# Storing a quarter of the output's rows in one transfer instead of four

## The chip, the cores and the metric

The kernel runs on one core of a Trainium2 chip. The core has a matrix engine (PE, with a separate row PEld for its weight loads), a vector engine (DVE), a scalar engine (ACT), GpSimd (POOL) and SyncE (SP). Data between the chip's buffers and DRAM moves through 16 DMA engines, which serve transfers issued from the queues of SP, ACT and POOL.

The metric is device time in microseconds of one execution. The profile is of one execution, and its span reaches from the first to the last instruction of the program.

## The reference

The kernel mixes two long convolutions of the same input with a gate. Shapes: one sequence of 2048 positions with 448 channels, bf16.

```python
x = A_u                                             # (1, 2048, 448)
g = sigmoid((x * gate_w).sum(-1, keepdims=True))    # a gate for each position
# A: state-space convolution; its kernel K is made from 256 complex modes a channel
K = einsum("dn,dnl,dn->dl", C, exp(dt * A * l), dt * B).real
a = irfft(rfft(x, 4096) * rfft(K, 4096))[:2048] + x * Dskip
# B: shifted keys times values, convolved with a given kernel, times x
kv = shift4(k, shift_k) * v
b = x * (irfft(rfft(kv, 4096) * rfft(ssm_k, 4096))[:2048] + kv * ssm_D)
return g * a + (1 - g) * b                          # (1, 2048, 448)
```

## The kernel before, in words

The two convolutions are done as Fourier transforms written as matrix products on PE. The 448 channels are held as 4 groups of 112; the work goes through four parts H = 0 to 3, each with 28 channels of every group. `PLAN` gives the order of the parts' steps: tables for the kernel of A (`table`), the convolution B (`conv_B`), the convolution A (`conv_A`), and the mixing of a finished part (`mix`). Parts 0 to 2 end in `mix`; part 3 ends in `end`, which also stores the output.

The order of the instructions is written out by hand. All calls on the engines are recorded in a list (`Order`), and `issue` replays them in the order that the string `ORDER` names by number; on each engine the instructions stand in that order. Since every call is replayed from line 144, nearly all rows of the profile carry L144, and groups are told apart by the names of their tiles. The strings `SLOTS` and `ROOMS` say which buffer each temporary uses, and `SIDES` says whether a copy out of PSUM is done by DVE (a TENSOR_SCALAR) or by ACT (an ACTIVATE).

The output's 2048 rows are seen as 32 x 4 x 16, named a, x and y: row = 64a + 16x + y. Two buffers called `lines`, each of 128 partitions, collect finished rows. Partition 32x + a holds, for that a and x, eight values of y with 448 channels each: `lines[0]` has y from 0 to 7 (q_82 in the program), `lines[1]` has y from 8 to 15 (q_80). So a partition's four neighbouring values of y are 4 x 448 x 2 = 3,584 bytes that are contiguous in the buffer and in the output.

`mix` fills the columns of parts 0 to 2. `end` goes over h = 0, 1 (the buffer) and k = 0, 1 (the half of its eight values of y). Each of the four passes does the last products of A on PE, gates and adds on DVE (tile RK), turns the result to the output's order on PE (`relay`, 16 small products), copies it out of PSUM with a change of sign (`evac.minus`), and stores that quarter of the rows. In the order as replayed the quarters are finished as h=1 k=0, then h=0 k=1 and h=1 k=1, then h=0 k=0; ACT does the copy of the first three, DVE that of the last.

The stores are issued from `dmae`, a list of SP and ACT. A store waits for the copies that write its rows, and nothing waits for a store but the end of the program. Every transfer signals on one of eight semaphores that are used in turn for SP's and ACT's transfers, and a transfer that takes up a semaphore waits for the transfer that used it before.

Of the kernel before, what the change touches and what calls it, by code (L numbers as in the profile page):

```python
# [110 lines left out]
)  # L111

def after(tc, ins, before):
# [55 lines left out]
def shaped(flat, shape, dtype=bf16, at=0):  # L169
    n = 1  # L170
    for s in shape:
        n *= s
    ap = flat if dtype is flat.dtype else flat.bitcast(dtype)
    ap = ap[:, at:at + n]
    names = "abcde"[:len(shape)]
    return ap.rearrange("p (%s) -> p %s" % (" ".join(names), " ".join(names)), **dict(zip(names, shape))) if len(shape) > 1 else ap
# [524 lines left out]
class Modes:  # L701
# [5 lines left out]
    def across(self, nm, put):  # L707
        for hf in range(2):
            for g in range(4):
                put(hf, g, self.raw[nm][:, g, hf * 128:(hf + 1) * 128])  # L710
# [36 lines left out]
def body(  # L747
# [22 lines left out]
    dmae = [nc.sync, nc.scalar]  # L770
# [143 lines left out]
    for b0 in range(0, 64, 8):  # L914
        pt = places.room()
        for i in range(2):
            for d in (0, -1, 1, -2, 2, -3, 3):
                t0 = b0 + 4 * i + d
                j0, j1 = max(0, -d), min(4, 4 - d)
                for g in range(4):  # L920
                    x = kT[g][:, t0 % 16, 2 + t0 // 16:2 + t0 // 16 + 4 * 31 + 1:4]
# [35 lines left out]
    out_rows = out[0].rearrange("(a x y) l -> x a y l", a=32, x=4)  # L957
    lines = []

    def line(y0):  # L960
        if not lines:
            lines.extend(qt([8, 448]) for _ in range(2))
        return lines[y0 // 8][:, y0 % 8:]

    def relay(o, g, part, first, last):
        for x in range(4):
            nc.tensor.matmul(o[32 * x:32 * x + 32].rearrange("p (y c) -> p y c", c=NC), lhsT=minus[:, 32 * g:32 * g + 32], rhs=part(x),
                             start=first, stop=last, tile_position=(0, 32 * x))

    def laid(t, H):  # L970
        return t.rearrange("p y (g h c) -> p h g y c", g=4, c=NC)[:, H]
# [8 lines left out]
    def end(U, H):  # L980
        across = lambda t, y0, n: t.rearrange("p (x y) c -> p x y c", x=4)[:, :, y0:y0 + n]
        for h in range(2):
            for k in range(2):
                ps, pt = (places.room()[:, 0] for _ in range(2))
                y0 = 8 * h + 4 * k
                b = across(ug[H], y0, 4)
                nc.tensor.matmul(ps[:, 0:448].rearrange("p (x y c) -> p x y c", x=4, c=NC), lhsT=minus[:], rhs=b, start=True, stop=False)
                for i in range(16):
                    for r in range(2):
                        l = 16 * (i // 4) + y0 + i % 4  # L990
                        nc.tensor.matmul(ps[:, i * NC:(i + 1) * NC], lhsT=G[:, l, r].rearrange("p g a -> p (g a)"), rhs=U[:, r, l],
                                         start=False, stop=(r == 1 and i == 15))
                t = shaped(arena["RK"][:], [4, 4, NC], at=448 * (2 * h + k))
                V.tensor_tensor(out=t, in0=ps[:, 0:448].rearrange("p (x y c) -> p x y c", x=4, c=NC),
                                in1=gt[:].rearrange("p (x y) -> p x y", x=4)[:, :, y0:y0 + 4].unsqueeze(3).to_broadcast([P, 4, 4, NC]), op=ALU.mult)
                V.tensor_tensor(out=t, in0=t, in1=b, op=ALU.add)
                for g in range(4):
                    relay(pt[:, 112 * g:112 * g + 112], g, lambda x: t[:, x], g == 0, g == 3)
                evac.minus(laid(line(y0)[:, 0:4], H), pt[:, 0:448].rearrange("p (g y c) -> p g y c", g=4, c=NC))
                for x in range(4):  # L1000
                    dmae[x % 2].dma_start(out_rows[x][:, y0:y0 + 4], lines[h][32 * x:32 * x + 32, 4 * k:4 * k + 4])

    held_open = []

# [50 lines left out]
    def conv_A(what, H, K):  # L1055
        X = spread_in(lambda c: uu[:, :, H * NC + c])
        transform(nc, places, W2, X, evac)
        X, S = swapped(X)
        if H < NQG - 1:
            transform(nc, places, W2, K, evac)  # L1060
            conv(products(nc, X, S, K), what, H)
            return
        U = qt([2, 64, NC])
        for c0 in (0, CB):
            transform(nc, places, W2, K, evac, c0, c0 + CB)
            for k0 in (0, 16):
                products(nc, X, S, K, k0, k0 + 16, c0, c0 + CB)
            stage_a(nc, places, R, whole(U, evac), (X, S), [range(c0, c0 + 8), range(c0 + 8, c0 + CB)])
        end(U, H)
# [57 lines left out]
```

## Time and profile before

| | before |
|---|---|
| time, median of 3 runs | 247.13 us (246.75 to 247.59) |
| the profiled execution | 248.35 us |
| its span | 246.4 us |
| PE busy / DVE busy / ACT busy | 209.4 / 228.4 / 220.4 us |
| DMA packets, bytes | 43,347, 26.27 MB |
| stores of the output | 16 of 112 KB, 8 on SP's queue and 8 on ACT's |
| time from issue to landing of a store | 2.1 us at least, 3.1 median, 3.7 at most |

The busy times are unions over the span, and matrix products overlap their weight loads. For a store the profile has the short time of the issuing instruction on its queue, and separately the packets that the DMA engines moved; "GB/s" and "DMA share" of a window count these packets. A DMA share of 1 means that all 16 DMA engines were busy; a packet is counted in the window in which it starts, so that a short window can show a little over 1.

### The profile page before, as it was taken

The numbers are of one execution on the slowest core, as the hardware profiler recorded it, in microseconds if no ns is written. First come the engines' busy times: TensorE is split into PE (matmuls) and PEld (weight loads), VectorE is DVE, ScalarE is ACT, GpSimd is POOL, SyncE is SP. The second block draws the span as 40 slices with busy tenths as digits, with TensorE's granted clock in tenths as the row PEclk, the third lists the DMA queues.
The fourth block names the chain that finished last, engine by engine and source line by source line (L and its number), as shares of the span: only waits on it lengthen the run. The fifth ranks groups of instructions, "written<-read, shape, count | busy, mean of one in ns | idle before, by whom it ended". The sixth has DMA issues, their size and how long they took to land.

```text
span 246.4 us, 12201 instructions
## 1 busy us (share of the span) xinstructions
PE 209.4 (85%) x5451; PEld 185.5 (75%) x5451; DVE 228.4 (93%) x394; ACT 220.4 (89%) x333; POOL 39.9 (16%) x112
## 2 busy tenths in 40 slices
PE   0747699877999998887899988979999999999970
PEld 0645277566988988787889977978989998998850
DVE  7999999999686999999999999999999999989870
ACT  5999999998999999999999999989999997586640
POOL 8700002030002141000011450001434102000000
PEclk9999799999999999999999999999999999999985
DMA  5997999993103498000688680000775402300035
GB/s 131 306 184 155 238 203 192 187 195 79 23 5 78 116 228 168 7 5 3 92 118 152 142 215 24 7 3 11 125 132 155 114 5 68 89 4 3 3 115 186
DMA packets 43347, 26.27 MB, mean 107 GB/s; under 512 B 34144, under 2 KB 40256, under 8 KB 43296
## 3 DMA queue, kind: packets, MB, share of 16 engines
q1 hardware_dynamic: 38848, 15.64, 30.9%
q0 software_dynamic: 3600, 8.95, 18.0%
q8 instruction: 42, 0.69, 1.2%
q10 hardware_dynamic: 848, 0.92, 1.1%
q14 instruction: 9, 0.07, 0.1%
HBM read 9.78 MB, written 2.87 MB: 51 GB/s over the span
## 4 chain that ended last, share of the span: by engine, by line
PE 36%; DVE 23%; ACT 19%; DMA 7%; issue 7%; SPq 4%; POOL 0%; DVEq 0%; ACTq 0%; POOLq 0%
PE ps L144 36%; ACT q L144 15%; DVE TP L144 10%; DVE TQ L144 5%; SPq L144 4%; DVE q L144 4%; ACT G L144 3%; DMA natu<-in_A_u_dram 3%; DMA gw<-in_gate_w_dram 2%; DMA TP<-TP 2%; DMA q<-in_B_ssm_k_dram 1%; DVE RK L144 1%; DVE ET L144 1%; DVE G L144 1%; DVE natv L144 1%
## 5 line engine op out<-in xcount | busy, mean ns | idle before, releaser
L144 ACT CAST q<-ps 128x896 bf16<-128x896 f32 (+4 forms) x172 | 133.2, 900 | 11.1 <-PE ps L144 10.6
L144 PEld LDWEIGHTS <-q 128*128 128x128 bf16 (+2 forms) x784 | 41.0, 134 | 8.9 <-issue 3.8
L144 PEld LDWEIGHTS <-G 128*128 128x128 bf16 (+2 forms) x1136 | 35.5, 103 | 15.3 <-issue 7.2
L144 DVE TENSOR_TENSOR TQ<-TQ,ET 128x896 bf16<-128x896 bf16 (+2 forms) x70 | 45.4, 682 | 0.1
L144 PE MATMUL ps<-q,s_W 128*128 128x112 bf16 (+1 forms) x544 | 33.5, 210 | 3.8 <-ACT q L144 2.1
L144 PE MATMUL ps<-sa_R,q 128*128 128x128 bf16 x448 | 33.6, 229 | 3.3 <-issue 1.7
L144 PE MATMUL ps<-TP,TQ 128*32 128x32 bf16 x1792 | 32.9, 240 | 2.1 <-issue 1.8
L144 PEld LDWEIGHTS <-s_W 128*128 128x128 bf16 x544 | 27.6, 97 | 7.6 <-issue 4.9
L144 PEld LDWEIGHTS <-TQ 128*32 128x32 bf16 x1792 | 29.9, 153 | 4.2 <-issue 2.3
L144 DVE TENSOR_TENSOR q<-q,q 128x3584 bf16<-128x3584 bf16 (+1 forms) x22 | 32.3, 1508 | 0.6 <-ACT q L144 0.6
L144 POOL DMA_DIRECT2D TP<-TP x15 | 13.4, 895 | 112.0 <-PE ps L144 64.8
L144 DVE TENSOR_TENSOR TP<-TP,ET 128x1792 bf16<-128x1792 bf16 (+3 forms) x25 | 31.5, 1269 | 0.1
L144 ACT ACTIVATE q<-hold 128x224 bf16<-128x224 f32 (+1 forms) x81 | 28.7, 410 | 0.1
L144 POOL DMA_DIRECT2D q<-q x30 | 16.1, 564 | 56.2 <-ACT q L144 30.2
L144 PEld LDWEIGHTS <-natu 128*64 128x64 bf16 (+1 forms) x288 | 21.5, 206 | 4.8 <-DMA natu<-in_B_k_dram 3.6
L144 PE MATMUL ps<-q,G 128*128 128x56 bf16 (+1 forms) x640 | 20.3, 182 | 1.0 <-ACT q L144 0.9
L144 ACT ACTIVATE ET<-q 128x1344 bf16<-128x1344 int16 (+1 forms) x12 | 17.3, 1477 | 0.0
L144 PE MATMUL ps<-Wc,natu 128*64 128x128 bf16 x224 | 16.5, 284 | 0.5 <-ACT q L144 0.5
L144 PE MATMUL ps<-Wc,natv 128*64 128x128 bf16 x224 | 16.1, 285 | 0.6 <-ACT q L144 0.6
L144 PEld LDWEIGHTS <-natv 128*64 128x64 bf16 x224 | 15.2, 213 | 1.5 <-issue 1.0
L144 DVE TENSOR_TENSOR TQ<-TQ 128x448 bf16<-128x448 bf16 (+2 forms) x35 | 15.3, 443 | 0.2
L144 PE MATMUL ps<-G 112*32 112x336 bf16 (+3 forms) x448 | 14.0, 274 | 1.3 <-issue 0.7
(96 smaller groups left out, 280.0 us busy)
## 6 DMA issues: line engine op xcount, KB each, us to landing
TP<-TP POOLq DMA_DIRECT2D x9, 448.0 KB, 5.8
q<-q SPq DMA_DIRECT2D x34, 112.0 KB, 3.4
q<-q POOLq DMA_DIRECT2D x30, 112.0 KB, 4.0
natu<-in_B_k_dram SPq DMA_DIRECT2D x2, 896.0 KB, 10.3
q<-in_B_ssm_k_dram SPq DMA_DIRECT2D x16, 112.0 KB, 3.8
natv<-in_B_v_dram SPq DMA_DIRECT2D x8, 224.0 KB, 5.3
natu<-in_A_u_dram SPq DMA_DIRECT2D x8, 224.0 KB, 8.1
TP<-TP POOLq DMA_DIRECT2D x6, 224.0 KB, 3.6
```

The lines of the kernel that those rows point to most:

```text
L144: ins = f(*args, **kw)
```

## The change

For each of the four quarters, the loop over x with four stores of 32 partitions is replaced by one store of all 128 partitions. The four stores of a quarter were issued on SP and ACT in turn by x; the one store is issued on SP for k = 0 and on ACT for k = 1. The output's side of the store now has three dimensions, x (4), a (32) and 1,792 elements, where it had a (32) and 1,792; the buffer's side has 128 partitions where it had 32. The bytes that are stored and where they go stay the same.

```diff
-                for x in range(4):
-                    dmae[x % 2].dma_start(out_rows[x][:, y0:y0 + 4], lines[h][32 * x:32 * x + 32, 4 * k:4 * k + 4])
+                dmae[k].dma_start(out_rows[:, :, y0:y0 + 4], lines[h][:, 4 * k:4 * k + 4])
```

The string `ORDER` loses the twelve calls that are gone, and the numbers behind them move up. All other instructions keep their places on PE, DVE, POOL and ACT. On ACT, the second store (h=0 k=1) and the last one (h=1 k=1) stand right behind the copies that write their rows, and on SP the two stores stand last.

```diff
-    "5869-5876 6092 5901-5908 5877 5911-5918 6273-6305 5878 5919 5909 5920 6217-6249 5910 6306-6307 5890-5897 6250 "
-    "5880-5887 5898 6308-6323 6251 6161-6193 5899 6324 5888 6252-6267 5889 6194 6329-6361 6326-6327 6268 6325 6362 6272 "
-    "6269 6363 6270-6271 6195 6364-6379 6328 6196-6211 6380 6212 6381-6382 6216 6213 6215 6214 6383-6384 "
+    "5869-5876 6092 5901-5908 5877 5911-5918 6267-6299 5878 5919 5909 5920 6214-6246 5910 6300-6301 5890-5897 6247 "
+    "5880-5887 5898 6302-6317 6248 6161-6193 5899 6318 5888 6249-6264 5889 6194 6320-6352 6319 6265 6353 6266 6354 6195 "
+    "6355-6370 6196-6211 6371 6212 6372 6213 "
```

## The prediction

> **What bounds the kernel now.** I read the span and the queues on the page first, then the timeline of the last ten microseconds, the DMA traffic of that stretch, and last the waits of SyncE's queue. The profiled execution took 248.35 us with a span of 246.4 us. The median of the runs shown is 247.13 us, so the sum is made against 248.35 and carried over as a difference to 247.13.
>
> The timeline of the end, start and length in us:
>
> ```profile
> 236.34 0.54 ACT L144 ACTIVATE q<-ps 128x448 bf16<-128x448 f32 x1 [0.65 <-DVE q L144]
> ...
> 236.91 5.15 SPq L144 DMA_DIRECT2D out_dram<-q  x8
> 236.91 0.39 ACTq L144 DMA_DIRECT2D out_dram<-q  x1
> 237.35 0.54 ACT L144 ACTIVATE q<-ps 128x448 bf16<-128x448 f32 x1 [0.46 <-ACT q L144]
> ...
> 237.92 1.32 ACTq L144 DMA_DIRECT2D out_dram<-q  x3
> ...
> 239.29 0.54 ACT L144 ACTIVATE q<-ps 128x448 bf16<-128x448 f32 x1 [1.40 <-PE ps L144]
> 239.64 0.62 DVE L144 TENSOR_SCALAR q<-ps 128x448 bf16<-128x448 f32 x1 [0.67 <-PE ps L144]
> 239.87 3.00 ACTq L144 DMA_DIRECT2D out_dram<-q  x4
> ```
>
> All computing is over at 240.26 (239.64 + 0.62). The span runs another 6.1 us, and in it only stores move. The DMA packets from 236 to the end:
>
> ```profile
> DMA packets 768, 1.84 MB, mean 177 GB/s; under 512 B 256, under 2 KB 256, under 8 KB 768
> ```
>
> And the busy times by window (length, busy time of PE, its weight loads, DVE, ACT and POOL, granted clock, busy share of the 16 DMA engines, GB/s):
>
> ```profile
> 237.00:237.75 0.75, 0.58 (x24) 0.48 (x20) 0.13 (x1) 0.40 (x1) 0.00 (x0) 1.00 0.00 0
> 237.75:238.35 0.60, 0.00 (x0) 0.00 (x0) 0.57 (x2) 0.14 (x1) 0.00 (x0) 1.00 1.00 197
> 238.35:238.60 0.25, 0.00 (x0) 0.00 (x0) 0.25 (x2) 0.00 (x0) 0.00 (x0) 1.00 0.94 373
> 238.00:244.00 6.00, 0.86 (x32) 0.58 (x32) 1.56 (x4) 0.54 (x1) 0.00 (x0) 0.59 0.92 282
> 244.00:244.80 0.80, 0.00 (x0) 0.00 (x0) 0.00 (x0) 0.00 (x0) 0.00 (x0) 0.50 0.29 108
> 244.80:246.40 1.60, 0.00 (x0) 0.00 (x0) 0.00 (x0) 0.00 (x0) 0.00 (x0) 0.50 0.00 0
> ```
>
> Stores move from 237.75, 0.84 us after the first issue at 236.91, until 244.80. These 7.05 us carry 1.84 MB (16 stores of 112 KB, 1.835 million bytes). From 238 to 244 the sixteen engines are busy 92% of the time. So the end is set by moving the output; the issues are done by 242.87 (239.87 + 3.00). The 1.60 us behind the last byte are completion and the end of the program, and SyncE's wait shows what it is for:
>
> ```profile
> SPq L1122 <- DMA out_dram<-q: 3.0, 2, 2.7
> ...
> SPq L144 <- DMA out_dram<-q: 0.4, 2, 0.2
> ```
>
> **The change, part by part.** The built programs differ in these instructions alone (shape of the output's side):
>
> ```
> before  16 x  DMACopy out_dram<-q   32x1792      (SP 8, ACT 8)
> after    4 x  DMACopy out_dram<-q   4x32x1792    (SP 2, ACT 2)
> ```
>
> Bytes and row length stay: 512 rows of 3,584 bytes, the 768 packets less 256 small ones. Those 256 are 16 completions for each of 16 stores: each of today's stores, with 32 as its outer count, ran on all sixteen engines.
>
> *The outer count of the output's side goes from 32 to 4.* This is the term that decides. The trace of before has two transfers with an outer count of 4, on SyncE's queue:
>
> ```profile
> q1 hardware_dynamic: 38848, 15.64, 30.9%
> ...
> TP<-in_B_shift_k_dram SPq DMA_DIRECT2D x4, 0.9 KB, 2.6
> ...
> dB<-in_B_ssm_D_dram SPq DMA_DIRECT2D x1, 0.9 KB
> d<-in_A_Dskip_dram SPq DMA_DIRECT2D x1, 0.9 KB
> ```
>
> SyncE issues 97 transfers, which by their shapes move 37,320 rows. With 16 completions each the queue would have 37,320 + 97 x 16 = 38,872 packets; the page has 38,848. The 24 that lack are 12 for each of the two: they posted 4 completions, so they ran on 4 engines. (Neither has a time to landing, which is taken from sixteen completions; the equally small load with 112 rows has.) The new store has 128 as its outer count on the buffer's side and 4 on the output's. No transfer of before has sides that differ so. I take 4 engines, since an engine that is given whole outer steps of both sides can be given no less than one of the four blocks, and the built instruction keeps the 4 outermost. The Trainium skill, page DMA: Bandwidth & Descriptors, section Why a DMA increments its semaphore by 16 and not by 1, states that a copy is spread over the largest number of engines up to 16 that divides the outermost count of both sides. By that rule the store has 4 engines, and both queues use the same, lowest-numbered four. The two 4-row loads agree with it; that both queues take the same four no run here shows.
>
> *The time of 1.835 million bytes on four engines.* It is bounded by what one busy engine moved:
> - quickest: a store of 128 partitions in mid-kernel, on all sixteen. Its window:
>
> ```profile
> 30.20:31.20 1.00, 1.00 (x14) 0.35 (x16) 1.00 (x3) 0.38 (x2) 0.00 (x0) 0.69 1.01 416
> ```
>
>   416 / (16 x 1.01) = 25.7 GB/s an engine; four give 103 GB/s and 17.8 us.
> - slowest: the first 0.60 us of the output, 197 / (16 x 1.00) = 12.3 GB/s; four give 49 GB/s and 37.3 us.
> - between: 238 to 244, 282 / (16 x 0.92) = 19.2 GB/s; four give 76.6 GB/s and 23.9 us. The burst from 238.35 to 238.60, at 373 / (16 x 0.94) = 24.8, shows that the same rows can go nearly at the upper rate.
>
> I take 19.2: it is from the same rows, from the same two queues at once, held for 6 us, while the others last a microsecond or less. The output then takes 23.9 us in place of 7.05: **+16.9 us**.
>
> Why the slow row could be the true one: the Trainium skill, page SBUF — State Buffer, section Door 1: The DMA port swizzle, states that partitions 32 apart share a DMA port. Four engines that walk the four blocks of 32 partitions side by side would stand on two ports, two engines to each. The trace agrees as far as it goes: the first store out, 32 partitions on sixteen engines, ran at half the rate of the 128-partition one. The sum by the rule is that of the second rival.
>
> *Twelve issues less.* ACT's queue loses six of its eight issues (4.71 us for eight: 0.39 + 1.32 + 3.00), SyncE's six of eight (5.15 us for eight), and its two waits for an earlier store's completion, 0.4 us. ACT's evacuation at 237.35 stood behind ACT's first issue (0.39 us) and starts about 0.4 us earlier, so the second store is issued at about 237.5 instead of 237.92. On the path this is worth nothing: the four engines have the first quarter's rows from 237.75 on. Without that cover it would be worth at most 0.4 us.
>
> *One issue of 128 rows in place of one of 32.* Today's issues of 32 rows take:
>
> ```profile
> L144 SPq DMA_DIRECT2D out_dram<-q x8: 315/362/558, 236.9 to 241.5; - x8
> L144 ACTq DMA_DIRECT2D out_dram<-q x8: 321/408/773, 236.9 to 242.1; - x8
> ```
>
> If the time grew with the rows, it would be 4 x 0.36 = 1.4 us, 1.1 us more before the first byte; if it doesn't, nothing. I take nothing, and the 1.1 us goes into the range.
>
> *Later quarters.* The stores are ready at 236.9 (SyncE), 237.5 and 239.83 (ACT), 240.26 (SyncE). The first two quarters alone keep four engines at 76.6 GB/s for 12.0 us, until 249.7, so the third and fourth are waiting when their turn comes. What is behind them on ACT's and SyncE's queues is only the end of the program. An ACT held up by its own full queue would delay the evacuation of 239.29, with some 10 us of slack. PE, DVE and POOL run the same instructions in the same order, and none reads the output.
>
> *Sum.* First byte 237.75, last byte 261.65, then 1.60: span 263.25 against 246.4, profiled execution 265.2 against 248.35. Against the median of 247.13 that is **264.0 us**.
>
> **Rivals.**
> 1. *All sixteen engines (faster).* The outer count of the buffer's side, 128, decides. For it: 128 rows are there to be dealt out, and the 128-partition store above ran at 416 GB/s. Against it: the two 4-row loads. A quarter of 458,752 bytes then takes 1.1 us at 416 GB/s; the last is issued at 240.3, moves from 241.1, stands behind the third (240.7 to 241.8) and ends at 242.9: 1.9 us saved, 245.2 us. At 282 GB/s the output ends at 237.75 + 6.5 = 244.25: 0.55 us saved, 246.6. I put it at 245.8. The point from which it decides: more than 13.6 engines at 19.2 GB/s (4 x 23.9 / 7.05).
> 2. *Four engines, two to a port all the way.* 37.3 us instead of 7.05: +30.2, 277.4 us. For it: 12.3 GB/s in the first 0.60 us, where sixteen engines worked on one block of 32 partitions. Against it: 24.8 GB/s right after, with rows of a second queue. Two queues stand at different rows, so the engines can be apart.
> 3. *Each queue on four engines of its own.* ACT's half, 917,504 bytes from about 238.3 at 76.6 GB/s, ends at 250.3: +5.5, 252.6 us. For it: nothing in the trace says which four a transfer takes. Against it: nothing there says that they are dealt out in turn either.
> 4. *No change that can be measured*: sixteen engines at a rate that loses again what the issues save, 247.1 us.
>
> **How the numbers follow.** Four engines at a rate between the bounds: 0.63, at 264.0, its own range 257.9 (17.8 us for the bytes) to 269 (29 us, at 15.8 GB/s an engine, midway between 19.2 and 12.3). Two to a port: 0.17. Two sets of four: 0.06. Sixteen: 0.11. No change: 0.03. The range that holds the first two, 0.80, goes from 257.5 to 278.5: its upper end is 277.4 and the 1.1 us of a longer issue. Faster by over 0.3% (0.7 us, about what a measurement of this kernel can tell): 0.11; within 0.3%: 0.03; slower: 0.86.
>
> **What would show it.** In the changed kernel, from 237.75 on: a DMA busy share of 0.25 and about 77 GB/s (103 at most, 49 at least) where it was 0.92 and 282; 16 completion packets at the end, four for each store, where there were 256; computing over at about 240.3 as now; and SyncE waiting some 20 us for the output. Wrong at the first step: 64 completions or a share near 0.9. Wrong at the rate: the share 0.25, but the end far from 261.7. Wrong on the queues: a share of 0.5. Wrong on the cover: gaps in the DMA share between 238 and the end.

## The result and the profile after

The changed kernel takes 262.14 us (261.64 to 262.84), against 247.17 us for the kernel before beside it: a ratio of 1.0611, 95% interval 1.0581 to 1.0641. The prediction was 264.0 us, in a range from 257.5 to 278.5.

The profiled execution took 262.44 us. Its timeline at the end, start and length in us:

```profile
236.45 3.75 SPq L144 DMA_DIRECT2D out_dram<-q  x2
236.89 1.15 ACTq L144 DMA_DIRECT2D out_dram<-q  x1
...
238.70 0.54 ACT L144 ACTIVATE q<-ps 128x448 bf16<-128x448 f32 x1 [1.84 <-PE ps L144]
239.00 0.62 DVE L144 TENSOR_SCALAR q<-ps 128x448 bf16<-128x448 f32 x1 [0.48 <-PE ps L144]
239.27 0.63 ACTq L144 DMA_DIRECT2D out_dram<-q  x1
```

Computing is over at 239.62, and all four stores are issued by 240.2. What follows is the output on its way, in windows (the columns are those of the windows of before; the last two are the busy share of the 16 DMA engines and GB/s):

```profile
237.00:237.73 0.73, 0.13 (x6) 0.02 (x1) 0.57 (x1) 0.00 (x0) 0.00 (x0) 1.00 0.00 0
237.73:242.25 4.52, 0.68 (x32) 0.47 (x32) 1.38 (x4) 0.54 (x1) 0.00 (x0) 0.88 0.26 50
242.25:256.25 14.00, 0.00 (x0) 0.00 (x0) 0.00 (x0) 0.00 (x0) 0.00 (x0) 0.50 0.26 103
256.25:259.26 3.01, 0.00 (x0) 0.00 (x0) 0.00 (x0) 0.00 (x0) 0.00 (x0) 0.50 0.15 61
259.26:260.70 1.44, 0.00 (x0) 0.00 (x0) 0.00 (x0) 0.00 (x0) 0.00 (x0) 0.50 0.00 0
```

The share of 0.26 is four engines of sixteen. Before, the same bytes went at a share of 0.92 and 282 GB/s. Two things were not in the prediction's sum: for the first 4.5 us the four busy engines move only 50 GB/s, half of what they move later, and at the end half the rate is gone for 2.4 us, as two engines run out of rows before the other two (from 256.90 to 259.26 the share is 0.12 and the rate 50 GB/s). The packets from 236 to the end, with the completions, and SyncE's wait:

```profile
DMA packets 529, 1.85 MB, mean 75 GB/s; under 512 B 16, under 2 KB 16, under 8 KB 528
```

```profile
SPq L1121 <- DMA out_dram<-q: 19.1, 3, 7.3
```

Sixteen completions for four stores, where 256 for sixteen stores stood before: four engines a store instead of sixteen.

The spans differ by 14.3 us (260.7 and 246.4), and the rows account for it. From the first to the last byte it is 21.53 us in place of 7.05: +14.5. The first byte comes 1.28 us after the first issue and not 0.84: +0.4. In this execution the first issue happens to come 0.46 us earlier, and the end behind the last byte is 0.16 us shorter.

### The profile page after: what moved, and what is told of

Its sections match the earlier page's. It is cut to its first block, busy times and chain, and to the rows that moved or that the text cites. A ratio compares the mean times of both kernels' runs of the same rounds, so it can differ in the third digit from the quotient of the medians.

```text
span 260.7 us, 12181 instructions
## 1 busy us (share of the span) xinstructions
PE 209.7 (80%) x5451; PEld 186.6 (72%) x5451; DVE 228.5 (88%) x394; ACT 220.1 (84%) x333; POOL 39.9 (15%) x112
## 4 chain that ended last, share of the span: by engine, by line
PE 30%; ACT 26%; DVE 19%; issue 7%; DMA 6%; SPq 2%; POOL 1%; DVEq 0%; ACTq 0%; POOLq 0%
PE ps L144 30%; ACT q L144 23%; DVE TP L144 5%; DVE q L144 4%; DVE TQ L144 3%; DMA q<-q 3%; DVE natv L144 2%; DMA natv<-in_B_v_dram 2%; SPq L144 2%; ACT G L144 1%; DMA q<-in_B_ssm_k_dram 1%; POOL q L144 1%; DVE ET L144 1%; DVE G L144 1%; ACT RK L144 1%
## 5 line engine op out<-in xcount | busy, mean ns | idle before, releaser
L144 PEld LDWEIGHTS <-q 128*128 128x128 bf16 (+2 forms) x784 | 41.6, 135 | 7.6 <-issue 3.3
L144 PEld LDWEIGHTS <-G 128*128 128x128 bf16 (+2 forms) x1136 | 34.9, 102 | 14.8 <-issue 6.8
L144 PEld LDWEIGHTS <-natu 128*64 128x64 bf16 (+1 forms) x288 | 22.1, 211 | 7.0 <-DMA natu<-in_B_k_dram 5.4
```

The lines of the kernel that those rows point to most:

```text
L144: ins = f(*args, **kw)
```

## The experiments

The theory to be tested (A): the outer count of the output's side sets the number of engines, and with it the time. The rivals: one issue of 128 rows is slow in itself (B), or something other than the outer count confines it (C). A second question came with the profile after: why the first 4.5 us were slow. Each kernel ran beside the kernel before on the same chip, which there took 248.4, 249.2 or 248.1 us (the three groups e1 to e4, e5 to e8, e9 to e11). e2, e3 and e5 to e9 were run once, and in the second group the kernel before too; single runs of the kernel before lie between 246.1 and 250.3 us, so a difference of 2 us between two such runs says nothing by its time alone.

### The same four stores, with an outer count of 128 (e1)

```diff
-                dmae[k].dma_start(out_rows[:, :, y0:y0 + 4], lines[h][:, 4 * k:4 * k + 4])
+                dmae[k].dma_start(out[0].rearrange("(p y) l -> p y l", y=16)[:, y0:y0 + 4], lines[h][:, 4 * k:4 * k + 4])
```

> The changed kernel, but the four stores write 128 evenly spaced rows each, so that the output's side has an outer count of 128 and not 4; bytes, row length, queues and order stay, and the rows land in other places than the reference's. Theory A (the outer count sets the number of engines): sixteen engines, 64 completions, a DMA share near 0.9 and over 350 GB/s while several stores are waiting; the output is out by about 243 and the time is 245.2 to 246.6 us, under the kernel before. Rival B (one issue of 128 rows is slow in itself, whatever engines it gets): about 262 us, as the changed kernel. Rival C (the four engines are real, but the outer count of the buffer's side, 128, would have given sixteen as well, so something else confines them): again about 262 us with a share of 0.25.

Measured: 246.66 us, a ratio of 0.9941 to the kernel before (0.9913 to 0.9969). The packets of the end, and the windows of the first two quarters and of the last two:

```profile
DMA packets 577, 1.85 MB, mean 34 GB/s; under 512 B 64, under 2 KB 64, under 8 KB 576
```

```profile
238.22:239.35 1.13, 0.17 (x16) 0.17 (x17) 1.09 (x3) 0.00 (x0) 0.00 (x0) 1.00 1.00 400
239.35:240.48 1.13, 0.51 (x32) 0.30 (x20) 0.65 (x2) 0.54 (x1) 0.00 (x0) 1.00 1.01 403
241.05:243.47 2.42, 0.00 (x0) 0.00 (x0) 0.00 (x0) 0.00 (x0) 0.00 (x0) 0.71 0.94 372
```

64 completions for four stores: sixteen engines. The number of issues, the buffer's side, the bytes and the queues are those of the changed kernel; the 15 us that it lost are gone, and 1.5 us more. The rows land in other places, and both sides now have the same shape; what each of these does is taken up with e2 and e8. B and C fall. This is also what the change could have brought with a layout whose rows lie evenly spaced: some 1.5 us.

### Outer counts of 8 and 2 (e2, e3)

```diff
+                dmae[k].dma_start(out[0].rearrange("(a b y) l -> b a y l", b=8, y=16)[:, :, y0:y0 + 4], lines[h][:, 4 * k:4 * k + 4])
```

> The changed kernel with an outer count of 8 on the output's side (8 blocks of 16 partitions; the rows land in other places than the reference's). Theory A: eight engines, 32 completions, a DMA share of 0.5 and about 205 GB/s; 64 rows an engine at 137 ns are 8.8 us in place of 7.05, so about 249 us, up to 251 if the first microseconds go as slowly as in the changed kernel. Rival B: about 262 us.

```diff
                 for x in range(4):
-                    dmae[x % 2].dma_start(out_rows[x][:, y0:y0 + 4], lines[h][32 * x:32 * x + 32, 4 * k:4 * k + 4])
+                    if x % 2:
+                        nc.calls.append((None, (), {}))
+                    else:
+                        dmae[x // 2].dma_start(out_rows[x:x + 2, :, y0:y0 + 4], lines[h][32 * x:32 * x + 64, 4 * k:4 * k + 4])
```

(A call of `None` is passed over when the order is replayed, so that the numbers in `ORDER` still hold; e6, e9 and e10 use the same.)

> Two stores of 64 partitions for each quarter, the output's side with an outer count of 2, the first on SyncE, the second on ACT. Theory A: two engines, 16 completions, a DMA share of 0.13 and about 52 GB/s; 256 rows an engine at 137 ns are 35 us, so 275 us, up to 283 with a slow start. Rival B (the size of the store decides): between the kernel before and the changed one, 247 to 262 us.

Measured: 254.46 us with an outer count of 8 and 279.17 us with 2. The windows of e2, then of e3:

```profile
238.83:242.00 3.17, 0.94 (x32) 0.69 (x32) 1.33 (x4) 0.54 (x1) 0.00 (x0) 0.58 0.51 103
242.00:250.93 8.93, 0.00 (x0) 0.00 (x0) 0.00 (x0) 0.00 (x0) 0.00 (x0) 0.50 0.45 169
```

```profile
238.02:242.00 3.98, 0.68 (x32) 0.47 (x32) 1.41 (x4) 1.09 (x2) 0.00 (x0) 0.66 0.12 27
242.00:275.74 33.74, 0.00 (x0) 0.00 (x0) 0.00 (x0) 0.00 (x0) 0.00 (x0) 0.50 0.13 51
```

Shares of 0.5, 0.26 and 0.13 for outer counts of 8, 4 and 2; e2 has 32 completions for four stores and e3 16 for eight, so eight and two engines a store. From the first to the last byte it takes 12.1, 21.5 and 37.7 us. Smaller stores (e3 has eight of 224 KB) made it worse, as A says. e2 came out 3.5 us over the upper end of its estimate. The kernel before was 1.2 us slower on that chip; most of the rest is that its bytes took 12.1 and not 8.8 us. Its start is slow too, from 245.80 to 249.20 its eight engines fall back to 177 GB/s (197 before that), and from 249.20 on some have run out of rows (a share of 0.23).

### Ports: the two queues on different halves of the buffer (e4)

```diff
-                    dmae[x % 2].dma_start(out_rows[x][:, y0:y0 + 4], lines[h][32 * x:32 * x + 32, 4 * k:4 * k + 4])
+                    dmae[x // 2].dma_start(out_rows[x][:, y0:y0 + 4], lines[h][32 * x:32 * x + 32, 4 * k:4 * k + 4])
```

> The kernel before with one change: of the four stores of a quarter, SyncE issues x = 0 and 1 and ACT issues x = 2 and 3, where they took turns. Theory P (the stores of partitions 0 to 63 share one half of the buffer's ports, those of 64 to 127 the other, and before, both queues worked on the same half at the same time): the rate from 238 to 244 goes from 282 GB/s to 350 or more, the output is out 0.5 to 1.9 us earlier, 245.3 to 246.7 us. Rival (ports don't matter, the rate is set elsewhere): 247.2 us, 282 GB/s.

Measured: 248.34 us, a ratio of 0.9990 (0.9959 to 1.0021): no difference. Its stores moved at 279 GB/s from the first to the last byte, 6.6 us:

```profile
236.07:242.65 6.58, 0.94 (x32) 0.70 (x32) 1.82 (x4) 0.68 (x2) 0.00 (x0) 0.57 0.88 279
```

The rate of the stores of 32 partitions isn't lifted by this.

### The slow start: four engines on neighbouring blocks, and on blocks 32 partitions apart (e5, e9)

Both have four engines a store. In e5 the blocks are 8 partitions of one store of 32; in e9 they are 16 partitions of one store of 64, so that two pairs of blocks lie 32 partitions apart.

```diff
 e5 (sixteen stores)
+                    dmae[x % 2].dma_start(out_rows[x].rearrange("(a b) y l -> b a y l", b=4)[:, :, y0:y0 + 4], lines[h][32 * x:32 * x + 32, 4 * k:4 * k + 4])
 e9 (eight stores, x = 0 and 2)
+                        dmae[x // 2].dma_start(out[0].rearrange("(c p y) l -> c p y l", c=2, y=16)[x // 2].rearrange("(a b) y l -> b a y l", b=4)[:, :, y0:y0 + 4],
+                                               lines[h][32 * x:32 * x + 64, 4 * k:4 * k + 4])
```

> The kernel before with its sixteen stores of 32 partitions, but each with an outer count of 4 on the output's side (4 blocks of 8 partitions, which lie on different ports; the rows land in other places than the reference's). Both theories have four engines: 64 completions for the 16 stores, a DMA share of 0.25. They differ in the first microseconds, which in the changed kernel went at half the later rate. Theory P (there, two engines walked the partitions of one port in step): no slow start, 104 GB/s from the first row on, 17.5 us from the first to the last byte, the kernel before plus 10.5 us, some 258 to 259 us where the kernel before is at 247.2 to 248.4. Rival D (the rows of a store whose two sides have different shapes are dealt out slowly, whatever ports they are on): a slow start as in the changed kernel, 20 us or more, 261 to 263 us.

> Two stores of 64 partitions for each quarter, each with an outer count of 4 on the output's side: four engines with blocks of 16 partitions, of which the first and third, and the second and fourth, lie on the same ports (the rows land in other places than the reference's). The stores of 32 partitions on four engines, with no shared ports, took 19.0 us from the first to the last byte, the changed kernel, with shared ports, 21.5; 512 rows at 137 ns on four engines are 17.5. Theory P (the second slow group of rows comes from shared ports): two engines of the four have a second group of four slow rows, 600 ns or more each, and the bytes take 20.5 to 22 us. Rival (something else in the 128-partition store, its size or its 32 rows an engine): only the first four rows are slow, 18 to 19.5 us.

Measured: 260.63 us for e5 and 262.67 us for e9. The windows of e5, then of e9:

```profile
238.20:239.50 1.30, 0.68 (x32) 0.47 (x32) 0.82 (x3) 0.54 (x1) 0.00 (x0) 1.00 0.25 50
239.50:242.20 2.70, 0.00 (x0) 0.00 (x0) 0.49 (x1) 0.49 (x1) 0.00 (x0) 0.73 0.26 104
242.20:257.22 15.02, 0.00 (x0) 0.00 (x0) 0.00 (x0) 0.06 (x1) 0.00 (x0) 0.50 0.25 99
```

```profile
238.33:242.00 3.67, 0.68 (x32) 0.47 (x32) 1.39 (x4) 1.09 (x2) 0.00 (x0) 0.67 0.28 54
242.00:259.23 17.23, 0.00 (x0) 0.00 (x0) 0.00 (x0) 0.00 (x0) 0.00 (x0) 0.50 0.24 96
```

e5 fits neither theory: it does start slowly, but for 1.3 us and not for 4.5, and its bytes take 19.0 us, between 17.5 and 20. e9, with blocks 32 partitions apart, is slow for 3.7 us, and its bytes take 20.9 us, as the port theory said. e5 also goes slow again, at 72 GB/s from 242.20 to 243.50. So a slow start is there without blocks 32 partitions apart.

The longer slow stretch of e9 doesn't show the ports either, since e9 differs from e5 in the size of its blocks as well. Over the runs so far, e6 to e8 and the changed kernel, the length goes with the number of rows that an engine has of one store: 8 rows, 1.3 us (e5, e8); 16 rows, 3.2 to 3.7 us (e2, e9); 32 rows, 4.0 to 4.5 us (e3, e6, e7 and the changed kernel). e8, shown below, speaks against the ports: its blocks of 8 lie 32 partitions apart like those of e9, and yet it is slow for no longer than e5. The packets of the changed kernel don't fit them well: of the 59 rows that start in its slow 4.5 us, 28 took at most 150 ns, as later, and 12 took 542 to 1,045. Two engines that take turns on one port would make rows about twice as long (some 280 ns, an estimate from the 140), not some of them up to seven times and others not at all. The trace doesn't name the port that a packet uses, so a share of the ports isn't ruled out; what makes these rows slow stays open.

### The second queue (e6, e7)

```diff
 e6 (only the stores with k == 0 are left, both on SyncE)
+                if k == 0:
+                    dmae[k].dma_start(out_rows[:, :, y0:y0 + 4], lines[h][:, 4 * k:4 * k + 4])
 e7
-                dmae[k].dma_start(out_rows[:, :, y0:y0 + 4], lines[h][:, 4 * k:4 * k + 4])
+                dmae[0].dma_start(out_rows[:, :, y0:y0 + 4], lines[h][:, 4 * k:4 * k + 4])
```

> The changed kernel with SyncE's two stores only; ACT's two are left out, so half of the output isn't written. Four engines, 64 rows each. Theory P (ports) and D (shapes): the first store starts as slowly as in the changed kernel with ACT's stores gone, 8.8 us and 2 to 4 more from the first to the last byte. Rival Q (the issue of the second store on ACT's queue, 1.15 us long, holds up the rows of the first): no slow start, rows of 140 ns from the first on, the first store out in 4.4 us and the last byte 8.8 us after the first, or a little later because the last store is issued only 3.2 us after the first.

> The changed kernel with all four stores on SyncE's queue. If both queues use the same four engines, as the share of 0.26 in the changed kernel says, nothing is to be had from the second queue: the same 137 ns a row, 21 to 22 us from the first to the last byte and 261 to 263 us. If the second queue cost or saved something, the slow first microseconds change: 17.5 us (258 to 259 us in all) if the two queues hinder each other there.

Measured: 253.30 us for e6, half of the output, and 262.63 us for e7. The first window of e6, then of e7:

```profile
237.72:242.00 4.28, 0.87 (x32) 0.59 (x32) 1.39 (x4) 0.54 (x1) 0.00 (x0) 0.59 0.24 51
```

```profile
238.34:242.50 4.16, 0.68 (x32) 0.47 (x32) 1.39 (x4) 0.54 (x1) 0.00 (x0) 0.94 0.24 47
```

In e6 the first 4.3 us went at 51 GB/s with nothing on ACT's queue, so the issue on ACT isn't what holds up the first rows (rival Q falls). In e7 all four stores on one queue take 21.2 us from the first to the last byte, as on two queues, and the start is as slow. Both queues serve the same four engines, and the second is worth nothing here.

### The shape of the output's side (e8, e11), and stores of 64 rows (e10)

```diff
 e8
+                dmae[k].dma_start(out[0].rearrange("(a b y) l -> b a y l", b=16, y=16)[:, :, y0:y0 + 4], lines[h][:, 4 * k:4 * k + 4])
 e11
-                    dmae[x % 2].dma_start(out_rows[x][:, y0:y0 + 4], lines[h][32 * x:32 * x + 32, 4 * k:4 * k + 4])
+                    dmae[x % 2].dma_start(out_rows[x].rearrange("(a b) y l -> b a y l", b=16)[:, :, y0:y0 + 4], lines[h][32 * x:32 * x + 32, 4 * k:4 * k + 4])
 e10 (eight stores, x = 0 and 2)
+                        dmae[x // 2].dma_start(out[0].rearrange("(c p y) l -> c p y l", c=2, y=16)[x // 2][:, y0:y0 + 4],
+                                               lines[h][32 * x:32 * x + 64, 4 * k:4 * k + 4])
```

> The changed kernel with an outer count of 16 on the output's side (16 blocks of 8 neighbouring partitions; the rows land in other places than the reference's). Theory A: sixteen engines, 64 completions. Against the store of 128 evenly spaced rows, which also has sixteen, two things differ: the two sides have different shapes, and blocks 32 partitions apart lie on one port, two engines to each. Theory P: the first rows take 255 ns or more and not 140, a store takes 2 us or more instead of 1.1, the time is 246 to 249 us. If neither ports nor shapes matter: 140 ns a row and the time of the 128-row store, 246.7 us where the kernel before is at 248.4.

> The kernel before with its sixteen stores of 32 partitions on sixteen engines, two rows to each; only the shape of the output's side differs, 16 x 2 rows where it was 32 (the rows land in other places than the reference's). Theory D (a store whose two sides have different shapes is issued and started more slowly): the issue takes about 0.63 us and not 0.35, the first byte comes some 0.4 us later after the issue (1.25 and not 0.84), the first rows take up to 500 ns, and with 16 such issues the last byte comes 1 to 4 us later than in the kernel before. Rival (the count of engines is all that matters): the times of the kernel before within 0.5%.

e8, with sixteen engines that each take 8 neighbouring partitions, took 248.82 us beside 249.22 us, one run each. It has 64 completions. Its two sides differ in shape as in the changed kernel, and still the 15 us are gone: it is the outer count that costs them, and not the shape. Its first window shows all engines busy at half the rate that e1 had there; after it they move 358 GB/s for a microsecond (240.70 to 241.70), and from 242.40 to 243.60 they fall to 257:

```profile
239.44:240.70 1.26, 0.68 (x32) 0.47 (x32) 0.76 (x3) 0.28 (x1) 0.00 (x0) 1.00 1.01 205
```

e11, the kernel before with nothing but a two-dimensional output side on the same sixteen engines, took 249.10 us, a ratio of 1.0059 (1.0028 to 1.0089). Its issues (min/median/max in ns):

```profile
L144 SPq DMA_DIRECT2D out_dram<-q x8: 550/586/663, 236.8 to 242.5; - x8
L144 ACTq DMA_DIRECT2D out_dram<-q x8: 561/658/810, 236.8 to 242.8; - x8
```

Its first byte comes 1.3 us after its first issue, as in the changed kernel. So the shape alone lengthens an issue from 362 to 586 ns on SyncE and from 408 to 658 on ACT (medians), and costs 1.5 us over sixteen stores (0.7 to 2.2). Against the 15 us of the changed kernel it is small.

Stores of 64 evenly spaced rows, with SyncE on partitions 0 to 63 and ACT on 64 to 127:

> Two stores of 64 partitions for each quarter with 64 evenly spaced rows on the output's side, so sixteen engines and the same shape on both sides; SyncE has partitions 0 to 63, ACT 64 to 127 (the rows land in other places than the reference's). If the gain of the 128-row store over the kernel before (0.994) comes from having few, wide stores with the two halves of the ports busy at once, this has nearly all of it: 0.994 to 0.997 of the kernel before. If it comes from how a store of all 128 partitions is dealt out over the engines, rows here take 250 ns as in the stores of 32 partitions and the time is that of the kernel before.

Measured: a ratio of 1.0033 (0.9997 to 1.0069), 282 GB/s from the first to the last byte:

```profile
238.26:244.78 6.52, 0.68 (x32) 0.47 (x32) 1.49 (x4) 0.54 (x1) 0.00 (x0) 0.59 0.90 282
```

So it isn't few and wide stores that made e1 faster. e10 begins at 202 GB/s for 1.24 us and goes on at 300. e1 alone, with stores of all 128 partitions on evenly spaced rows, held 400 GB/s from the first row on (350 from the first to the last byte, with the wait for the third quarter in it).

## Why the prediction was right, and where its sizes were off

- *Four engines from an outer count of 4.* Right, and shown: 16 completions, a share of 0.26, and times that follow the outer count from 128 over 16 and 8 to 2. The Trainium skill, page DMA: Bandwidth & Descriptors, section Why a DMA increments its semaphore by 16 and not by 1, gives the rule, and all runs agree with it: the smaller of the two outer counts, 4 and not 128, was the one that decided. Both queues took the same four engines: while both had stores waiting, the share stayed at 0.26. The same section of the Trainium skill puts a transfer on the lowest-numbered engines, from which the same follows.
- *The time of the bytes*, the term that was mis-sized: 23.9 us at a rate of 19.2 GB/s an engine, measured 21.5 us. No such rate was held for long. For 14 us the engines went at the upper bound, 103 / (16 x 0.26) = 24.8 GB/s, and for the first 4.5 us at the lower one, 50 / (16 x 0.26) = 12.0. The rate taken from before was an average over sixteen engines with stores of 32 partitions, and that it came near the average of another fast and another slow stretch is luck as much as argument. The other terms came out small: the first byte came later and the end was shorter by less than half a microsecond each.
- *One issue of 128 rows.* Taken at nothing, with 1.1 us in the range; measured 0.63 us in place of 0.35 for the first issue (0.56 to 1.15 for all four) and a first byte 0.4 us later. e1 (0.34 to 0.37 us for 128 rows) and e11 (0.59 us for 32) show that the shape does it and not the rows.
- *Twelve issues less, and the earlier second store.* Worth nothing, as said: the four engines were behind by then.
- *The later quarters* were issued by 240.2 and waited for their engines; the DMA share has no gap until two engines run out at about 257.
- *Rival 1, sixteen engines,* is what e1 ran: 0.9941, some 1.5 us, where the rival's sum had 0.55 to 1.9.
- *Rival 2, two engines to a port all the way,* falls: its rate was there for 4.5 us and then not. The Trainium skill, page SBUF — State Buffer, section Door 1: The DMA port swizzle, would have partitions 32 apart share a port. That the rate is half at first fits, but e5 starts at half its rate without such blocks, e8 has them and is slow no longer than e5, and the slow rows of the changed kernel are few and very long. No record names a port, and why the start is slow stays open.
- *Rival 3, two sets of four,* falls with the share of 0.26 and with e7.

A faster kernel would need the 128 partitions in the order of the output's rows, (a, x) in place of (x, a). The products of `relay` write one x to each block of 32 partitions, so that it would take other products on PE; this wasn't tried. e4, which needs no new layout, gave nothing.

## What to carry to other kernels

Before several transfers are merged into one, look at the outermost count on both sides as the instruction has it, not at the bytes or the partitions: the smaller count can take engines away, and four stores on sixteen engines beat one store on four by 15 us here. The number of completion packets in the DMA view, and the busy share while only that transfer runs, tell how many engines it has. When a rate is taken over from another stage, ask whether it is one rate or an average over a slow and a fast stretch.

## What the runs showed of the hardware that was not expected

- One engine moved 24.8 to 26 GB/s with rows of 3,584 bytes outside the slow stretches, for 14 us on end in the changed kernel (four engines: 103 GB/s there, 104 in e5), and its rows then took 140 ns.
- Most of these ways to store began slowly, with their engines busy: 50 GB/s in place of 104 for 1.3 us in e5, 205 in place of 358 for 1.3 us in e8, 202 in place of 300 for 1.2 us in e10, 197 in place of 373 for 0.6 us in the kernel before. e1 did not. e10 and the kernel before have sides of equal shape, as e1 has, so the shape alone isn't the reason. In e2, e5 and e8 the rate fell again later. Why is left open.
- Stores of 32 and of 64 partitions on all sixteen engines moved 282 GB/s (before, from 238 to 244), 279 and 282 (e4 and e10, from the first to the last byte), with the queues taking turns or each on its half of the partitions; the stores of 128 partitions on evenly spaced rows moved 400.
